# Keys loaded ahead of queries, and 154 of the first 345 steps of a hand-ordered program moved

## The chip, the core and the metric

The kernel runs on one core of a Trainium2 chip. Its time is device microseconds of one execution; 244.88 us is the median of three runs (244.7 to 245.37). A profiled execution gives the trace that is read here.

## What is computed

Attention with squared sketches, and behind it a feed-forward block that multiplies two projections. Cut to its core:

```python
# q, k, v: (4, 4, 1088, 32); S1, S2: (8, 32)
def phi(x):
    a = np.einsum('rd,bhsd->bhsr', S1, x)
    b = np.einsum('rd,bhsd->bhsr', S2, x)
    return np.einsum('bhsi,bhsj->bhsij', a, b).reshape(*x.shape[:-1], 64)
q_p, k_p = phi(q), phi(k)
kv = np.einsum('bhsf,bhsd->bhfd', k_p, v)
z = np.sum(k_p, axis=2)
x = einsum('bhsf,bhfd->bhsd', q_p, kv) / (einsum('bhsf,bhf->bhs', q_p, z)[..., None] + 1e-6)
x = x.transpose(0, 2, 1, 3).reshape(4352, 128)
out = (((x @ w1) * (x @ w2)) @ w3) @ w_out        # w1, w2: 128 x 1024; w3: 1024 x 1024; w_out: 1024 x 128
```

S and the weights come as float64 words, which the kernel turns into float32 itself.

## The kernel before

The program is a list of 1179 named steps. `make_steps` defines each step as a function that issues a few instructions; the text `ORDER` names the steps one by one, and each engine (and each of the queues that issue DMAs, SP's and ScalarE's) gets its instructions in that order. An engine never passes an instruction that waits. Buffers are handed out in the same order: `SLOTS` says, tag by tag, which of the buffers each allocation takes, so a load into a buffer waits for the last reader of what was there. DMAs take eight completion counters in turn, and one that takes a counter again waits for the landing of its former user. Of the large loads at most four (`UNDER_WAY`) are outstanding.

Names: a prefix says whose step it is, then a dot, then what it does.

- `s.*`: the sketch matrices. `s.load`, `s.words` (ScalarE, L263 and L295), `s.pair`, `s.lead`, `s.sum` (DVE), `s.low`, `s.rest` (POOL), `s.T`, `s.P`, `s.R` (TensorE), `s.tc`, `s.Pc`, `s.c` (ScalarE); `s.blk` and `s.blkh` spread them over heads on POOL, into `RS` and `Rh`.
- `k0` to `k3`: keys of the four batches. `k0.load0` and `k0.load1` are issued on ScalarE's queue (two heads each), `k0.loadr` (the last 64 rows) on SP's. `max` is a sum of absolute values on ScalarE (L207) that sets a grid, `g` adds its two halves, `lead` rounds to the grid (L214 on DVE, L211 and L212 on ScalarE), `rest` subtracts (L651). `tr` transposes (TensorE, L685), `kT` copies the transposed keys, `ab` and `abc` make the sketches, `kp` their products (L677). `gram0` to `gram4` add up keys' inner products in `ps_g` (L659). From it, `Gm`, `Gt`, `Ga`, `Gb`, `Gc`, then `T0`, `T1`, `Ta`, `Tb`, `Tc`, then `N0`, `N1`, `Na`, `Nb` find the denominator's matrix, alternately on TensorE and DVE; `Nh` and `Nf` spread it over heads (POOL). `kv0` to `kv3` and `kvr` add up kv in `ps_kv` (L769, L776); `kvm`, `kzt`, `kz`, `kvc`, `kqt`, `kq` bring it into the forms that queries meet.
- `kr0`, `kr1`: the last 64 rows of keys of two batches at a time.
- `q0` and `q1`: the first two groups of 512 queries (batch 0). `tr` (DVE, L1000) turns them, `restT` takes the remaining columns (L979), `max`, `l2`, `l1` (ScalarE) and `rm` (DVE) cut them into two parts. `A0`, `C0` (numerator side) and `A1`, `C1` (denominator side) are products; `C1` of `q0` gives `ps_cy`, which `C1t` turns into `ay_C` (L1068). `sm`, `st`, `sh`, `sl`, `sc` with a or y, `al`, `p01`, `p2`, `p12`, `dn`, `de`, `rc` end in `s_rc`, one over the denominator; `phi`, `pt`, `pc`, `x`, `xc`, `xs`, `xt`, `xT` make the group's `xT`.
- `w0` to `w10`: weights; `load`, `c` and `m` on ScalarE, `j` on DVE, `a` on POOL.
- `g0` to `g7`, `gr`: the feed-forward block by groups of 512 tokens: `a` and `b` (TensorE, L1799 and L1809), `c` (copy, L1804), `m` (product, L1815), `o`.
- `warm0` to `warm11`: products of zeros with zeros (L255), `WARM` gives their counts. They keep TensorE at work while it has nothing else.

An fp32 product is two matmuls and two weight loads on TensorE; one of zeros (bf16) is one of each.

Of the kernel before, what the change touches and what calls it, by code (L numbers as in the profile page):

```python
# [72 lines left out]


ORDER = """
c.zeros warm0 q0.load c.ident s.four c.act c.mask s.zero k0.zero v0.zero s.load k0.load0 k0.loadr q0.restT q0.tr
k0.load1 s.words kr0.load k0.tr1 s.pair s.low s.lead s.sum k0.max0 k0.max1 warm1 q0.max k0.tr0 warm2 kr0.tr kr0.kT
warm3 s.rest w1.load s.T s.P s.tc warm4 q0.l2 k0.kT1 s.Pc s.R k0.g k0.lead0 s.c s.blk k0.rest0 q1.tr k0.gram0 s.blkh
k1.zero s.Pm warm5 q0.l1 q0.A0 warm6 kr0.ab k0.lead1 q0.rm q0.sma q0.sta warm7 k0.kT0 v0.load v0.loadr k1.load k0.ab1
q0.sha k0.rest1 q0.C0 k0.gram1 k0.gram2 k0.gram3 k0.gram4 k0.ab0 k0.abc1 q1.max q0.C0t q0.sla q1.l2 k1.loadr s.Pp  # L80
k0.Gm k0.Gt k0.Ga w1.c1 k0.Gb k0.abc0 k0.T0 q1.l1 warm8 kr0.abc k0.kp1 q0.sca w1.j1 k0.Ta k0.kp0 k0.Gc w1.c0 k1.tr0
kr1.load k2.zero k1.tr1 k1.kT1 kr0.kp warm9 k0.N0 warm10 k0.Na warm11 k0.T1 k0.kv0 k0.Tc k0.Tb k0.N1 k0.Nb k0.Nh q1.rm
q0.al k0.Nf q0.phi0 q0.phi1 q0.A1 q0.smy w1.m1 k1.max q0.sty q0.shy k0.kv3 k0.kv1 k0.kv2 q0.sly s.KS k0.kvr kr1.tr
k0.kvm w1.m0 kr1.kT q0.p01 q1.C0 q1.C1 q0.C1 k0.kzt k2.loadr q0.pt0 q0.C1t q0.scy q0.p2 k0.kz q0.pt1 k0.kvc kr1.ab
k0.kqt q0.p12 q0.dn q0.de q0.rc w1.j0 q0.pc0 q0.pc1 q0.x0 k1.kT0 q0.x1 q0.xs0 q0.xs1 q0.xt0 w1.a0 q1.A0 k2.load
w0.load k1.lead0 q0.xc0 q0.xc1 k0.kq w1.a1 k2.max q0.xt1 k1.ab q0.xT0 q0.xT1 g0.4a q1.load g0.5a q1.sm w0.m1 q1.st
q1.Ct g0.4c g0.4b q1.sh q1.sl k1.rest0 g0.7b w0.c1 g0.7a k1.abt w0.j1 k1.gram0 w0.c0 s.RC q1.scy k1.gram1 kh2.load
q1.sca q2.tr g0.5c q1.al q1.p01 q1.p2 k1.gram2 k1.gram3 kr1.abc k1.gram4 w6.load w0.m0 g0.6b w0.j0 g0.7c g0.7m k1.Gm
q1.p12 k1.Gc g0.0a w2.load w0.a1 q1.dn q1.de q1.rc q1.bs k1.Gt g0.3a k1.Ga k1.T0 k2.kT1 k1.Gb g0.3c q1.restT g0.2a
q1.phi k1.T1 q1.pt0 g0.4m w0.a0 q2.max q2.l2 g0.6a k1.Ta k2.lead0 k2.rest0 g0.1a g0.2c k1.Tc g0.5b q3.tr g0.5m k1.Tb  # L90
q1.pc0 q1.pt1 g0.1b w9.load k1.N0 s.AR q2.l1 q2.rm v3.zero q1.pc1 k1.N1 q1.x g0.6c g0.1c k1.Na k1.Nr k3.zero k2.gram0
g0.1m k2.gram1 k2.gram2 q3.max k2.gram3 g0.0c k2.kT0 k1.Nb q1.xT k2.gram4 q3.l2 k2.ab q2.A0 q2.C0 q2.C1 q3.l1 k1.kp0
v1.zero w9.c k2.abt g1.5a g1.5c g1.1a q2.Ct g1.7a q2.At q3.rm q3.A0 k0.Nr q2.sm q3.C0 q3.C1 k2.Gm v1.loadr q2.st w2.m
q2.sh g1.1c g1.2a k1.kp1 g0.6m q3.Ct g1.0a g1.7b k3.load v1.load g1.5b q3.At k2.Gt k3.loadr w2.c k2.Ga g0.0b w9.j
q2.sl g1.7c w6.c g1.6a k1.kv0 q3.sm k2.Gb w5.load q2.sc q2.al g1.0c k2.Gc g1.7m q2.p01 q3.st k1.kv2 k1.kv3 q3.sh w9.m
k1.kv1 k2.T0 k1.kvr q3.sl q2.p2 k2.T1 q2.p12 q2.dn q2.de g1.4a q2.rc k3.max g0.3b g0.0m g1.1b kh3.load g1.4c k2.Ta
g1.2b q3.sc g1.2c w5.c k2.Tc k1.kvc k1.kqt k1.kq g0.3m q3.p01 g1.6c g1.3a g1.5m g1.3b q2.bs q2.phi0 q2.pT0 g1.2m g1.3c
q2.x q2.load k2.N0 k2.Tb k3.lead0 w9.a1 k2.N1 g1.4b q3.al q3.p2 q3.p12 q2.xT0 g2.5a k3.kT1 g2.5c g2.6a q3.dn q3.de
# [51 lines left out]
def make_steps(ctx, tc, q, k, v, S1, S2, moe_w1, moe_w2, moe_w3, moe_w_out, out):  # L150
    nc = tc.nc
    dve, act, pe, pool, sp = nc.vector, nc.scalar, nc.tensor, nc.gpsimd, nc.sync
    B, H, S, D = q.shape
# [96 lines left out]
    def warm(name, times, tag="out"):  # L250
        @step(name)
        def _():
            t = ps(tag, [128, 256], "idle_ps")
            for _ in range(times):
                pe.matmul(t, zeros, bview(zeros, [[0, 2], [1, 128]]), start=True, stop=True)  # L255

# [586 lines left out]
    def k_end(b):  # L843
        a = acc[b]
        tag = "t"

# [63 lines left out]
        def by_head(o, P, x, start, stop):  # L910
            for h in range(H):
                pe.matmul(o[h * D:(h + 1) * D], P, a["Tp"][:, x, h], start=start, stop=stop,
                          tile_position=(0, h * D), skip_group_check=True)
# [1021 lines left out]
```

## Time and profile before

| | |
|---|---|
| median of three runs | 244.88 us (244.7 to 245.37) |
| profiled execution, span | 244.1 us |
| instructions in the span | 6745 |
| TensorE, DVE, ScalarE, POOL busy | 97%, 85%, 51%, 66% |
| moved by DMA | 22.06 MB, mean 90 GB/s |

The span runs from the first to the last instruction of one execution; the page gives no other time of that execution. The runs' times include what lies ahead of the first and behind the last instruction: the median is 0.78 us above the span. The page has the engines' busy time, the span in 40 slices (6.1 us each), the DMA queues, and the chain that ended last; further answers of the trace give instructions in order of time, waits, and the sums of chosen stretches (for each engine busy time, and in brackets the count of instructions).

### The profile page before, as it was taken

The numbers are of one execution on the slowest core, as the hardware profiler recorded it, in microseconds if no ns is written. First come the engines' busy times: TensorE is split into PE (matmuls) and PEld (weight loads), VectorE is DVE, ScalarE is ACT, GpSimd is POOL, SyncE is SP. The second block draws the span as 40 slices with busy tenths as digits, with TensorE's granted clock in tenths as the row PEclk, the third lists the DMA queues.
The fourth block names the chain that finished last, engine by engine and source line by source line (L and its number), as shares of the span: only waits on it lengthen the run. The fifth ranks groups of instructions, "written<-read, shape, count | busy, mean of one in ns | idle before, by whom it ended". The sixth has DMA issues, their size and how long they took to land.

```text
span 244.1 us, 6745 instructions
## 1 busy us (share of the span) xinstructions
PE 236.2 (97%) x2724; PEld 129.8 (53%) x2724; DVE 206.7 (85%) x421; ACT 123.5 (51%) x246; POOL 161.9 (66%) x203
## 2 busy tenths in 40 slices
...
GB/s 201 265 143 325 181 227 190 6 197 224 220 141 251 188 217 190 59 1 3 3 0 0 4 0 3 59 113 3 1 0 0 0 3 0 0 1 3 12 90 93
DMA packets 31935, 22.06 MB, mean 90 GB/s; under 512 B 21280, under 2 KB 26528, under 8 KB 31904
## 3 DMA queue, kind: packets, MB, share of 16 engines
...
q8 instruction: 21, 0.34, 0.6%
...
q14 instruction: 10, 0.08, 0.1%
...
## 4 chain that ended last, share of the span: by engine, by line
PE 87%; DMA 5%; ACT 2%; POOL 2%; DVE 1%; issue 1%; POOLq 0%; SPq 0%
PE b_ps L1809 12%; PE ps_o L1835 12%; PE ps_X L1673 11%; PE a_ps L1799 11%; PE ps_o L1759 10%; PE ps_w3o L534 6%; PE ps_Y L1673 6%; PE ps_Z L1673 3%; PE ps_g L659 2%; PE ps_x L1527 2%; PE ps_ac L1374 2%; DMA qh<-in_q_dram 2%; DMA k<-in_k_dram 2%; PE ps_or L1824 2%; POOL ph L1208 1%; PE idle_ps L255 1%
## 5 line engine op out<-in xcount | busy, mean ns | idle before, releaser
L1673 PE MATMUL ps_X<-xd,wv 64*128 64x512 f32 x112 | 36.3, 593 | 0.0
L1799 PE MATMUL a_ps<-xT,w 128*128 128x512 f32 (+1 forms) x80 | 36.1, 562 | 0.0
L1809 PE MATMUL b_ps<-xT,w 128*128 128x512 f32 (+1 forms) x80 | 35.6, 555 | 0.0
L1804 ACT COPY ffa<-a_ps 128x512 f32<-128x512 f32 (+1 forms) x38 | 20.1, 540 | 29.2 <-PE a_ps L1799 26.7
L1707 POOL TENSOR_TENSOR hc<-hc 128x512 f32<-128x512 f32 x16 | 20.7, 1304 | 15.7 <-DVE hc L1685 15.5
L1835 PE MATMUL ps_o<-ab,w3o 128*128 128x512 f32 x64 | 29.6, 600 | 0.0
L1680 ACT COPY hc<-ps_X 128x512 f32<-128x512 f32 x38 | 21.3, 590 | 16.1 <-PE ps_X L1673 12.9
L1815 DVE TENSOR_TENSOR ab<-ffa,b_ps 128x512 f32<-128x512 f32 (+1 forms) x40 | 23.9, 623 | 4.9 <-PE b_ps L1809 4.1
L501 POOL TENSOR_TENSOR w3c<-w3c,cv_m 128x512 int32<-128x512 int32 x16 | 21.2, 1344 | 4.2 <-DVE w3c L495 4.1
L1673 PEld LDWEIGHTS ps_X<-xd,wv 64*128 64x128 f32 x112 | 14.9, 186 | 13.1 <-issue 10.9
L1799 PEld LDWEIGHTS a_ps<-xT,w 128*128 128x128 f32 x80 | 14.1, 189 | 13.9 <-issue 8.8
L1809 PEld LDWEIGHTS b_ps<-xT,w 128*128 128x128 f32 x80 | 14.4, 190 | 13.1 <-issue 8.1
L1673 PE MATMUL ps_Y<-xd,wv 64*128 64x512 f32 x48 | 19.7, 594 | 0.0
L1835 PEld LDWEIGHTS ps_o<-ab,w3o 128*128 128x128 f32 x64 | 11.6, 190 | 13.4 <-issue 13.0
L534 PEld LDWEIGHTS ps_w3o<-wo,w3T 128*128 128x128 f32 x128 | 15.3, 192 | 2.4 <-issue 2.4
L534 PE MATMUL ps_w3o<-wo,w3T 128*128 128x128 f32 x128 | 15.7, 276 | 0.0
L1759 PE MATMUL ps_o<-hc,w3o 128*64 128x512 f32 x32 | 15.1, 595 | 0.0
L1759 PE MATMUL ps_o<-tt,ws 128*64 128x512 f32 x32 | 13.7, 594 | 0.0
L1680 ACT COPY hc<-ps_Y 128x512 f32<-128x512 f32 x14 | 8.1, 592 | 9.7 <-PE ps_Y L1673 6.6
L263 ACT ACTIVATE cv_c<-raw 128x1024 f32<-128x1024 f32 (+1 forms) x13 | 13.0, 1014 | 0.0
L1540 ACT COPY xd<-ps_x 64x256 f32<-64x256 f32 x24 | 8.8, 367 | 7.2 <-PE ps_o L1835 6.8
...
## 6 DMA issues: line engine op xcount, KB each, us to landing
...
```

Source lines behind the costliest of these rows:

```text
L263: act.activation(dst, hi.bitcast(F32), ACT.Prelu, scale=2.0 ** -112, alpha=-2.0 ** 32)
L501: pool.tensor_tensor(d, d, x["m"][:, i * 512:(i + 1) * 512], ALU.add)
L534: pe.matmul(t["o"], w3T[ko][:, c], wo[:, c], start=c == 0, stop=c == NC - 1)
L1673: pe.matmul(x[bank], stat(j, u)[:, i * 128:(i + 1) * 128], rows(j, u), start=new, stop=True, tile_position=(u * 64, 0), skip_group_check=True)
L1680: cp(n(y))(x[k], x[bank])
L1707: on(f"h{g}.{i}m{k}").tensor_mul(both[0][k], both[0][k], both[1][k])
L1759: pe.matmul(acc_o[bank][half[0]:half[1]], w(i), x(i), start=n == 1, stop=n == (2 if j == 3 else 4), tile_position=(0, half[0]), skip_group ...
L1799: pe.matmul(x["a"][:, :w], w_of(0, c), xT[g][:, c0:c0 + w], start=True, stop=True)
L1804: cp(f"g{g}.{c}{su}c")(x["s"][:, :w], x["a"][:, :w])
L1809: pe.matmul(x["b"][:, :w], w_of(1, c), xT[g][:, c0:c0 + w], start=True, stop=True)
L1815: dve.tensor_mul(ab_sb[g, c][:, c0:c0 + w], x["s"][:, :w], x["b"][:, :w])
L1835: pe.matmul(o_ps[g], w3o[:, c], ab_sb[g, c], start=n == 1, stop=n == NC)
```

## The change

The order of the steps up to the 345th of 1179 is another one; none is added or taken out. Keys of batch 0 are loaded first, queries of batch 0 behind S. The zero products ahead of everything become 44 of 32 weight columns by 96 columns, instead of 27 of 128 by 256. `SLOTS` is rewritten so that buffers follow the new order. The list `CPV` loses three names whose steps are DVE transposes either way, and `two`'s users no longer write a name that `T1` and `N1` write. The diff, with the middle of the order cut:

```diff
-WARM = [27, 2, 3, 4, 4, 4, 1, 2, 1, 1, 2, 2]
+WARM = [44, 2, 3, 4, 4, 4, 1, 2, 1, 1, 2, 2]
...
 ORDER = """
-c.zeros warm0 q0.load c.ident s.four c.act c.mask s.zero k0.zero v0.zero s.load k0.load0 k0.loadr q0.restT q0.tr
-k0.load1 s.words kr0.load k0.tr1 s.pair s.low s.lead s.sum k0.max0 k0.max1 warm1 q0.max k0.tr0 warm2 kr0.tr kr0.kT
-warm3 s.rest w1.load s.T s.P s.tc warm4 q0.l2 k0.kT1 s.Pc s.R k0.g k0.lead0 s.c s.blk k0.rest0 q1.tr k0.gram0 s.blkh
-k1.zero s.Pm warm5 q0.l1 q0.A0 warm6 kr0.ab k0.lead1 q0.rm q0.sma q0.sta warm7 k0.kT0 v0.load v0.loadr k1.load k0.ab1
-q0.sha k0.rest1 q0.C0 k0.gram1 k0.gram2 k0.gram3 k0.gram4 k0.ab0 k0.abc1 q1.max q0.C0t q0.sla q1.l2 k1.loadr s.Pp
-k0.Gm k0.Gt k0.Ga w1.c1 k0.Gb k0.abc0 k0.T0 q1.l1 warm8 kr0.abc k0.kp1 q0.sca w1.j1 k0.Ta k0.kp0 k0.Gc w1.c0 k1.tr0
-kr1.load k2.zero k1.tr1 k1.kT1 kr0.kp warm9 k0.N0 warm10 k0.Na warm11 k0.T1 k0.kv0 k0.Tc k0.Tb k0.N1 k0.Nb k0.Nh q1.rm
-q0.al k0.Nf q0.phi0 q0.phi1 q0.A1 q0.smy w1.m1 k1.max q0.sty q0.shy k0.kv3 k0.kv1 k0.kv2 q0.sly s.KS k0.kvr kr1.tr
-k0.kvm w1.m0 kr1.kT q0.p01 q1.C0 q1.C1 q0.C1 k0.kzt k2.loadr q0.pt0 q0.C1t q0.scy q0.p2 k0.kz q0.pt1 k0.kvc kr1.ab
-k0.kqt q0.p12 q0.dn q0.de q0.rc w1.j0 q0.pc0 q0.pc1 q0.x0 k1.kT0 q0.x1 q0.xs0 q0.xs1 q0.xt0 w1.a0 q1.A0 k2.load
-w0.load k1.lead0 q0.xc0 q0.xc1 k0.kq w1.a1 k2.max q0.xt1 k1.ab q0.xT0 q0.xT1 g0.4a q1.load g0.5a q1.sm w0.m1 q1.st
+c.zeros warm0 k0.zero k0.load0 k0.loadr k0.load1 c.act s.load s.zero v0.zero c.ident s.four q0.load c.mask warm9
+s.words k0.max0 s.pair k0.tr1 warm1 s.lead s.low s.sum kr0.load warm4 k0.max1 k0.kT1 q0.tr w1.load s.rest warm5 s.P
+s.T kr0.tr s.tc k0.tr0 q0.max q0.restT k0.g s.R warm2 warm3 kr0.kT q0.l2 q1.tr k0.lead0 k0.rest0 s.c s.Pc k1.zero s.Pm
+q0.l1 k0.lead1 s.blk warm6 warm7 s.blkh kr0.ab q0.A0 q0.sma q0.sta k0.ab1 k0.gram0 q0.rm k1.load k0.rest1 v0.load
+q0.sha v0.loadr k0.gram1 q0.C0 k0.gram2 k0.gram3 k0.kT0 k0.abc1 k0.gram4 q1.max k0.ab0 q0.sla q1.l2 q0.C0t k1.loadr
+k0.Gm k0.Gt s.Pp w1.c1 k0.Ga k0.Gc warm8 k0.Gb k0.T0 kr0.abc q1.l1 k0.kp1 q0.sca k0.Ta w1.j1 k0.abc0 kr0.kp k0.Tb
+k0.T1 k0.kp0 w1.c0 kr1.load warm11 k1.tr1 k0.Tc k0.N0 k0.N1 warm10 k0.Na k1.kT1 k2.zero k1.tr0 k0.Nh k0.Nb k0.Nf q1.rm
+q0.al q0.phi0 kr1.tr q0.phi1 q0.A1 k0.kv0 k1.max q0.smy w1.m1 q0.sty k0.kv3 k0.kv1 q0.shy k0.kv2 q0.sly s.KS k0.kvr
+w1.m0 kr1.kT k0.kvm q0.C1 q1.C0 k0.kzt q0.C1t k2.loadr q0.pt0 q0.p01 q0.scy q0.pt1 k0.kz q0.p2 k0.kvc q0.p12 kr1.ab
+k0.kqt q0.dn q0.pc0 q0.de q0.rc w1.j0 w0.load q0.pc1 q0.x0 k1.kT0 q0.x1 q0.xs0 q0.xc0 q0.xt0 w1.a0 k2.load q0.xs1
+k0.kq w1.a1 q1.A0 q0.xt1 q0.xc1 q1.C1 k2.max k1.lead0 k1.ab q0.xT0 q0.xT1 g0.5a q1.load g0.4a q1.sm q1.st q1.Ct w0.m1
...
@@ the stretch of TensorE around the gram of batch 2
-q1.pc0 q1.pt1 g0.1b w9.load k1.N0 s.AR q2.l1 q2.rm v3.zero q1.pc1 k1.N1 q1.x g0.6c g0.1c k1.Na k1.Nr k3.zero k2.gram0
-g0.1m k2.gram1 k2.gram2 q3.max k2.gram3 g0.0c k2.kT0 k1.Nb q1.xT k2.gram4 q3.l2 k2.ab q2.A0 q2.C0 q2.C1 q3.l1 k1.kp0
+q2.l1 k1.Tb g0.1b g0.0c k1.N0 v3.zero w9.load s.AR k1.N1 g0.1c q2.rm k1.Na g0.6c q1.pc1 k1.Nr k3.zero k2.gram0 g0.1m
+k2.gram1 k2.gram2 q3.max q1.x k2.kT0 k2.gram3 k2.ab q1.xT q3.l2 k1.Nb g0.6m q3.l1 q2.A0 q2.C0 k2.abt k1.kp0 q2.C1
+g1.5a q2.Ct g1.1a g1.5c w9.c g1.0a q2.At k2.gram4 k0.Nr q3.rm q2.sm q3.A0 q3.C0 q2.st q3.C1 w2.m k2.Gm g1.7a q2.sh
...
         def _():
             t = ps(tag, [128, 256], "idle_ps")
+            if name == "warm0":
+                for _ in range(times):
+                    pe.matmul(t[:32, :96], zeros[:, :32], zeros[:, :96], start=True, stop=True)
+                return
             for _ in range(times):
                 pe.matmul(t, zeros, bview(zeros, [[0, 2], [1, 128]]), start=True, stop=True)
...
-            a["T"], a["Tr"] = two([D, H, r], "ps_T")
+            a["T"], rest = two([D, H, r], "ps_T")
+            if rest is not None:
+                a["Tr"] = rest
```

The same edit as the last stands in `N0`.

More of the change, by code (lines that the diff above doesn't have):

```diff
@@ L29 @@
     "b":
-        "012345670214657210671306537457462512346127340273014526045721472352140327540542370673245716"
+        "051226075314671250467315463470267152346127340270315426045721742351240327540642375072345716"
         "210605643174306437107523543106572361507514502371054643535436051532410354273245554744570504"
@@ L34 @@
     "l":
-        "0123456789a7486797c0864b7705995a34210b38c73b92bc0b4879c146a281ba56271a564b60303643a19ca32c"
+        "1023456879a7486797c0684b7705995a34210b38c73b92bc0b4879c146a281ba56271a564b60303643a19ca32c"
         "c2076b",
     "m":
-        "0123456789aejo96p3ke3rfjo7p5t8g50lfin6q8o4donmgp19fh2og3hi5601au6v4jm8emhubcusv62jgo6olsjs"
+        "2013456789aeoj9p63k3frejo7g5pt850qlifn68o4donmgp19fh2og3hi5601au6v4jm8emhubcusv62jgo6olsjs"
         "aolp8s0h8roj26gk1ivl8hb3mcu0a5pn7tfd9qe0umb4p5j1e2tkmgjeno5rcub7tjkume92fka4ud5tkbigpq10lv"
@@ L42 @@
     "raw": "010212120211221",
-    "s": "012345671252360063202461521024214",
-    "x": "012012201110",
+    "s": "012354671252360063202461521024214",
+    "x": "120012201110",
 }
-WARM = [27, 2, 3, 4, 4, 4, 1, 2, 1, 1, 2, 2]
+WARM = [44, 2, 3, 4, 4, 4, 1, 2, 1, 1, 2, 2]
 BY_PE = ()
@@ L65 @@
 CPV = set("""
-    g0.0c g0.1c h4.1ac h4.1ad h6.1bc h6.2ad k0.kT1 k1.kvc k2.kT1 k2.kq k3.kT0 k3.kT1 k3.kq q0.xc0
-    q0.xc1 q6.xT0 q6.xT2
+    g0.0c g0.1c h4.1ac h4.1ad h6.1bc h6.2ad k0.kT1 k1.kvc k2.kq k3.kq q0.xc0 q0.xc1 q6.xT0 q6.xT2
 """.split())
@@ L86 @@
-w0.load k1.lead0 q0.xc0 q0.xc1 k0.kq w1.a1 k2.max q0.xt1 k1.ab q0.xT0 q0.xT1 g0.4a q1.load g0.5a q1.sm w0.m1 q1.st
[L87 to L90, printed above, removed]
@@ L91 @@
-q1.pc0 q1.pt1 g0.1b w9.load k1.N0 s.AR q2.l1 q2.rm v3.zero q1.pc1 k1.N1 q1.x g0.6c g0.1c k1.Na k1.Nr k3.zero k2.gram0
-g0.1m k2.gram1 k2.gram2 q3.max k2.gram3 g0.0c k2.kT0 k1.Nb q1.xT k2.gram4 q3.l2 k2.ab q2.A0 q2.C0 q2.C1 q3.l1 k1.kp0
-v1.zero w9.c k2.abt g1.5a g1.5c g1.1a q2.Ct g1.7a q2.At q3.rm q3.A0 k0.Nr q2.sm q3.C0 q3.C1 k2.Gm v1.loadr q2.st w2.m
-q2.sh g1.1c g1.2a k1.kp1 g0.6m q3.Ct g1.0a g1.7b k3.load v1.load g1.5b q3.At k2.Gt k3.loadr w2.c k2.Ga g0.0b w9.j
-q2.sl g1.7c w6.c g1.6a k1.kv0 q3.sm k2.Gb w5.load q2.sc q2.al g1.0c k2.Gc g1.7m q2.p01 q3.st k1.kv2 k1.kv3 q3.sh w9.m
+c.zeros warm0 k0.zero k0.load0 k0.loadr k0.load1 c.act s.load s.zero v0.zero c.ident s.four q0.load c.mask warm9
```

9 lines of the change are left out of this document (8 added, 1 removed).

## The prediction

> **What bounds the kernel now.** I read the sums by engine first, then stretches of the span, then the chain of waits.
>
> ```profile
> PE 236.2 (97%) x2724; PEld 129.8 (53%) x2724; DVE 206.7 (85%) x421; ACT 123.5 (51%) x246; POOL 161.9 (66%) x203
> PE 87%; DMA 5%; ACT 2%; POOL 2%; DVE 1%; issue 1%; POOLq 0%; SPq 0%
> 30.00:60.00 30.00, 28.60 (x620) 15.43 (x619) 26.92 (x76) 20.17 (x38) 15.68 (x20) 1.00 0.67 169
> 60.00:100.00 40.00, 40.00 (x541) 22.54 (x541) 37.00 (x68) 24.08 (x43) 33.10 (x26) 1.00 0.81 198
> ```
>
> TensorE is busy all of 60 to 100 us; ahead of that it isn't, and all moved steps lie there. The 834 steps behind the moved ones are in the old order, so what arrives earlier at about 55 us should end the span earlier by as much. The question is how much earlier that is. Its first 30 us are set by a chain over all engines, so I follow that chain by rows of the timeline (start, duration, engine; in brackets the idle time ahead).
>
> ```profile
> 0.74 0.41 SPq L975 DMA_DIRECT2D qh<-in_q_dram  x1
> 0.98 0.95 ACTq L560 DMA_DIRECT2D k<-in_k_dram  x2
> 4.64 0.24 DVE L979 STREAM_TRANSPOSE qT_rest<-qh 128x64 f32<-128x64 f32 x1 [3.70 <-DMA qh<-in_q_dram]
> 4.81 0.67 DVE L1000 STREAM_TRANSPOSE qT<-qh 128x512 f32<-128x512 f32 x1
> 6.18 0.44 PE L685 MATMUL ps_kt<-ident,k 128*128 128x128 f32 x2 [0.28 <-DMA k<-in_k_dram]
> 6.41 0.68 ACT L207 ACTIVATE k_abs<-k 128x576 bf16<-128x576 f32 x1 [0.87 <-POOL sk_m L313]
> 7.76 0.61 ACT L207 ACTIVATE q<-qT 128x512 f32<-128x512 f32 x1
> 8.09 0.55 DVE L214 TENSOR_SCALAR kk<-k,k_g 128x512 f32<-128x512 f32 x1
> 8.66 0.69 DVE L651 TENSOR_TENSOR kk<-k,kk 128x512 f32<-128x512 f32 x1
> 9.27 0.70 DVE L1000 STREAM_TRANSPOSE qT<-qh 128x512 f32<-128x512 f32 x1
> 11.10 0.83 ACT L212 ACTIVATE kk<-kk,k_g 128x640 f32<-128x640 f32 x1
> 11.96 0.82 DVE L651 TENSOR_TENSOR kk<-k,kk 128x640 f32<-128x640 f32 x1
> 14.91 0.19 DVE L217 TENSOR_REDUCE G_g<-ps_g 128x1 f32<-128x32 f32 x1 [1.35 <-PE ps_g L659]
> 16.52 0.18 DVE L204 SCALAR_TENSOR_TENSOR T_p<-T_g,T_t 32x32 f32<-32x32 f32 x1
> 16.63 1.21 DVE L677 TENSOR_TENSOR kp<-kab 128x1024 f32<-128x1024 f32 x1
> 17.76 0.15 DVE L217 TENSOR_REDUCE N_g<-ps_N 128x1 f32<-128x8 f32 x1
> 18.96 0.16 DVE L937 TENSOR_TENSOR RC<-RC,ps_Nr 128x8 f32<-128x8 f32 x1 [0.41 <-PE ps_Nr L912]
> 19.20 0.67 POOL L949 TENSOR_TENSOR RS<-RC,mask 128x64 f32<-128x64 f32 x1
> 21.53 0.29 DVE L1097 TENSOR_TENSOR s_loy<-ps_ay,s_hiy 128x128 f32<-128x128 f32 x1
> 23.20 0.32 DVE L1068 STREAM_TRANSPOSE ay_C<-ps_cy 128x128 f32<-128x128 f32 x1 [1.38 <-PE ps_cy L1030]
> 25.55 0.71 ACT L1280 COPY xs<-s_rc 128x256 f32<-128x256 f32 x2
> ```
>
> Queries land at 4.64, keys at 6.18. ScalarE then works through keys' maximum (6.41), queries' maximum (7.76) and the second half of the keys' leading parts (to 11.93); DVE makes their rest (11.96), TensorE the gram, DVE the chain from G (14.91) to N (to 19.12), and the queries of group 0 wait 1.38 us for ps_cy.
>
> TensorE also has three waits put down to nothing but "issue". The next lines are instructions of TensorE counted from the start (products, then weight loads), pieces of the chain of waits around those waits, a row of the timeline, and two lines of the page:
>
> ```profile
> 0.00:13.80 13.80, 12.52 (x221) 10.28 (x221) 7.93 (x24) 9.07 (x23) 7.20 (x41) 1.00 0.85 239
> 0.00:19.45 19.45, 17.76 (x345) 14.54 (x346) 11.82 (x40) 13.25 (x33) 10.89 (x47) 1.00 0.75 214
> 0.00:45.80 45.80, 42.63 (x850) 29.05 (x851) 34.15 (x97) 32.71 (x74) 27.38 (x66) 1.00 0.75 205
> 12.07 0.79 PE ps_c L1030 x24
> 12.87 1.00 PE ps_g L659 x48
> 13.86 0.41 issue
> 14.27 0.58 PE ps_g L659 x23
> 20.35 0.69 PE L769 MATMUL ps_kv<-kp,v 128*32 128x64 f32 x34 [0.91 <-issue]
> 42.90 0.36 PE ps_N L912 x32
> 43.26 1.01 PE ps_x L1297 x4
> 45.83 1.16 issue
> q8 instruction: 21, 0.34, 0.6%
> GB/s 201 265 143 325 181 227 190 6 197 224 220 141 251 188 217 190 59 1 3 3 0 0 4 0 3 59 113 3 1 0 0 0 3 0 0 1 3 12 90 93
> ```
>
> They fall behind 221 + 221 = 442, 691 and 1701 instructions of TensorE: 249 apart, then 1010, which is four times 252. The instruction queue moved 0.34 MB in 21 packets, one per 16 KB. So code comes in blocks of some 250 instructions, and a block that is used up too fast costs a wait: 0.41 + 0.91 + 1.16 = 2.48 us in all.
>
> **Keys first (k0.load0, k0.loadr, k0.load1 ahead of q0.load).** The same bytes move, so the pair should end as now, at about 6.1; the first of it landed 4.64 - 0.74 = 3.9 us after its issue, so keys come at about 4.4 to 4.6, 1.6 earlier, and queries at 6.0, 1.4 later. k0.loadr stands ahead of S and q0 on SP's queue (small rows, 0.1 us or so); POOL's three fills ahead of ident cost it about 0.6 us, covered until the keys land. The keys' two maxima now run while ScalarE waits for queries (4.0 to 5.4 instead of 6.41 to 7.76). But q0.tr and q0.restT stand ahead of k0.g on DVE, and nothing there may pass them: q0.tr 6.0 to 6.65, restT to 6.85, k0.g 7.0, q1.tr (0.70) 7.65, lead0 8.2, rest0 8.9, where it ends at 9.35 now. ScalarE starts q0.max at 6.65 instead of 7.76; the same work follows, so k0.lead1 ends at 11.93 - 1.1 = 10.8. DVE's own queue ahead of k0.rest1 (q0.sma, sta, rm) is through at about the same time, an estimate; with 0.15 for it rest1 starts at 10.95 instead of 11.96. **Gain 1.0.**
>
> **Gram and G.** q0.C0 (48 of TensorE's instructions, 0.79 us on the chain) moves from ahead of gram1 to behind it, k0.gram0 behind k0.ab1: the sum is the same. gram1 starts 0.7 behind rest1's start, now (12.7) as then (11.65); 1.00 + 0.58 of gram and 0.79 of C0 follow, so the gram would end at 14.0. The first code wait comes at instruction 442 again, which is now the first product of gram3 instead of its middle, since the 17 further zero products (34 instructions) shift all that follows. It ended at 14.27. Its block is ordered once the one before is entered, now in k0.ab1, at 9.1 to 9.7 instead of some 9.5 to 10; so the wait ends about 0.3 earlier, at 14.0, with 96 instructions left instead of 58, some 0.7: end 14.7 if so, 14.0 if the block is there. I take the middle, 14.3, for the end and for Gm, which starts at 14.91 now. **Gain 0.6 stays** (between 0.2 and 0.9).
>
> **From G to N, and POOL.** k0.Ta ahead of w1.j1, k0.T1 and N1 right behind T0 and N0: N1 and Tb no longer stand between N0 and the end, but kp0 (1.2) still stands ahead of Na. From Ta's end (16.70) to RC's (19.12) it is 2.4 us now, with kp0, Na (0.6 with its shifts), Tb and two sums; then w1.j1 and Tb, 0.45, kp0 1.15, Na 0.58, the sums 0.3: 2.5. Nothing. Nf (0.67) moves ahead of q0.al on POOL, so phi0 on DVE, which needs al, starts 0.6 later. s_loy is thus ready at 21.82 - 0.6 + 0.6 = 21.8.
>
> **q0.C1 ahead of q1.C0, q1.C1 behind q1.A0.** ps_cy, made third of three now, is made first: 16 products, against 24 for C0's 0.79, so 0.5 us behind kvr. ps_cy is then there ahead of s_loy, and ay_C starts at 21.8 instead of 23.20. **Gain 1.4**: the idle 1.38 us go. If the second code wait ends as late as now (20.35), the kv products end at 21.1 and ps_cy is there at 21.7: still 1.4. If it ends 1 us later, 0.4 are left.
>
> **Queues that steps are moved past.** v0.load stands behind k1.load on SP, which waits for q1.tr (7.65 instead of 9.98). v0 lands behind w1 and k1: 2.1 MB from 6.1 on, at the 201 to 265 GB/s of the page's first two slices, is 14 to 16.5. kv0 starts at about 18: cover 1.5 us or more; without it, each us costs one. k2.load stands behind w0.load, and k2.max now ahead of k1.lead0 on ScalarE, so that a late k2 would hold up lead0, ffa and w0's words: it is wanted at 25.55 - 1.4 + 1.0 = 25.1, and w0 and k2, 1.6 MB at 265 to 325 GB/s from 16.5 at the latest, land by 22.6. Cover 2.5 us. k1.abt ahead of k1.rest0 on DVE fills the time that lead0 is later by. I cost these at nothing. The renamed buffers, the two rewritten helpers and the shorter list of copies change no instruction.
>
> **The third code wait.** By then 34 instructions more have been issued, and q1.x (1.01) stands behind gram2 instead of ahead of gram0. The block before is entered within N1 (0.36) instead of behind it, so the next comes some 0.4 earlier: 1.16 becomes 0.8. Bounds: it is gone (1.16), or it grows by as much as the longest wait seen (-1.16). I take 0.4. [...]
>
> **Zero products.**
>
> ```profile
> 1.00 4.69 PE L255 MATMUL idle_ps<-zeros 128*128 128x256 bf16 x27 [1.00 <-DVE zeros L229]
> 4.76 0.93 PE L255 MATMUL idle_ps<-zeros 128*128 128x256 bf16 x7
> ```
>
> Twenty of 27 start in the first 3.76 us, seven in the next 0.7: 0.19 to 0.21 us each, then about 0.11. So TensorE runs at half its pace until about 4.4, though the granted clock reads 1.00 in the rows from 0 on. A product of 96 columns is 96/256 of that, 0.08 us, and 44 of them end at about 4.5, as the keys land. Cost nothing, if the pace still changes at 4.4.
>
> **Sum.** 244.1 - 1.4 - 0.4 = 242.3 of span. The median of the runs, 244.88, is 0.78 above this profile's span: 243.1.
>
> **The rivals.**
> 1. The pace changes later. Products of 32 x 96 may not count as work, and behind 4.5 there is little to do until S's parts arrive. Each us that TensorE stays at half pace while it bounds the chain costs up to 0.5. The slow stretch was 3.4 us: one more costs up to 1.7 and gives 244.7; two more cost 3.4 and give 246.4, slower than before. It decides against the gain of 1.8 from 3.6 us on, so at a change behind 8.0. [...]
> 2. Code waits eat the early gain: the first as long as now with more behind it, the second 1 us longer, the third unchanged. 244.1 - 0.4 + 0.78 = 244.5. For it: the second block is fetched while v0, k2 and w0 load. Against: all is ordered earlier.
> 3. The third wait vanishes and queries land at 5.5: 244.88 - 1.9 - 1.16 = 241.8.
> 4. Nothing arrives, as another engine holds the stretch from 30 to 60: DVE is busy 26.92 of 30 there. But DVE too starts it earlier. 244.9.
>
> **How the numbers follow.** Forecast 0.50, 243.1 (242.3 to 243.9). Rival 3: 0.13. Rival 2: 0.13, at the edge between faster and same. Rival 1: 0.15, of which 0.08 with one stretch more (no change) and 0.07 with two. Rival 4: 0.09. A measurement of this kernel tells about 0.3% (0.7 us) from no change. Faster: 0.50 + 0.13 + half of rival 2 = 0.70; slower: 0.07 and 0.03 for a worse code wait = 0.10; same 0.20. The range leaves out two stretches of half pace and the best of rival 3: 241.5 to 245.2.
>
> **What would show it.** Right: keys' transposes at 4.5 and q0.tr at 6.0; G_g at about 14.3; no wait ahead of ay_C, which starts below 22; TensorE's waits for issue below 2.4 in sum; xs at about 24.2. Wrong: TensorE's zero products still 0.08 apart at 5 us, ScalarE waiting for k2 ahead of k1.lead0, kv waiting for v0, or a code wait over 1.5 us at a new place.

## The result, and the profile after

The changed kernel takes 248.78 us (median of 6 runs, 246.74 to 250.03) against 245.07 before; the ratio is 1.0143, interval 1.0108 to 1.0178. It is 1.4% slower, where 243.1 and faster was forecast. Times in this document are medians of all runs, and ratios compare fast runs alone (those within 1.5% of a kernel's shortest) with runs of the kernel before from the same round (medians 244.95 to 245.5), so the two differ a little where runs spread (e6, e10, e14, e18).

The page of the changed kernel: sums by engine, the granted clock in 40 slices, shares of the chain.

```profile
span 245.0 us, 6783 instructions
PE 236.0 (96%) x2741; PEld 130.6 (53%) x2741; DVE 207.0 (85%) x421; ACT 123.4 (50%) x246; POOL 161.6 (66%) x203
PEclk9997999999999999999999999999999999999999
PE 91%; DVE 3%; DMA 2%; issue 1%; SPq 1%; POOL 0%; ACT 0%; DVEq 0%
```

Two stretches of its span (busy time of each engine, then granted clock, DMA share, GB/s; a packet counts whole where it starts, so a share can pass 1):

```profile
30.00:60.00 30.00, 29.98 (x596) 15.90 (x598) 26.71 (x77) 21.42 (x38) 16.13 (x22) 1.00 0.71 172
60.00:100.00 40.00, 40.00 (x577) 22.50 (x566) 36.93 (x68) 24.10 (x43) 33.04 (x27) 1.00 0.84 211
```

From 30 us on TensorE hardly waits any more (29.98 of 30). The loss lies ahead of that, and there one slice of the clock reads 7. The chain's steps in the timeline of the changed kernel:

```profile
4.38 0.62 PE L688 MATMUL ps_kt<-ident,k 128*128 128x128 f32 x4
7.22 0.69 DVE L1007 STREAM_TRANSPOSE qT<-qh 128x512 f32<-128x512 f32 x1
8.05 0.18 ACT L349 COPY sk_t<-ps_st 32x32 f32<-32x32 f32 x1 [1.27 <-PE ps_st L344]
8.13 0.62 ACT L206 ACTIVATE q<-qT 128x512 f32<-128x512 f32 x1
11.26 0.83 ACT L211 ACTIVATE kk<-kk,k_g 128x640 f32<-128x640 f32 x1
12.20 0.88 DVE L654 TENSOR_TENSOR kk<-k,kk 128x640 f32<-128x640 f32 x1
12.91 1.98 POOL L680 TENSOR_TENSOR kp<-kab 128x1024 f32<-128x1024 f32 x1 [0.53 <-ACT kab L711]
12.99 2.04 DVE L203 SCALAR_TENSOR_TENSOR s_hla<-s_ga,s_t 128x128 f32<-128x128 f32 x1
15.73 0.28 PE L662 MATMUL ps_g<-kk 128*32 128x64 f32 x4 [1.78 <-issue]
16.56 0.19 DVE L216 TENSOR_REDUCE G_g<-ps_g 128x1 f32<-128x32 f32 x1 [0.85 <-PE ps_g L662]
21.00 0.16 DVE L944 TENSOR_TENSOR RC<-RC,ps_Nr 128x8 f32<-128x8 f32 x1
24.38 0.31 DVE L1075 STREAM_TRANSPOSE ay_C<-ps_cy 128x128 f32<-128x128 f32 x1
26.81 0.40 ACT L1287 COPY xs<-s_rc 128x256 f32<-128x256 f32 x1 [0.74 <-DVE s_rc L1205]
```

Keys are there at 4.38, as forecast, but the keys' leading parts end where they did (11.26 + 0.83), and in the gram TensorE waits 1.78 us for nothing but its own instructions, where it waited 0.41. Two stretches of 3.41 us around it; the clock's record changes at 17.44 and back at 20.85:

```profile
14.03:17.44 3.41, 1.71 (x56) 1.67 (x55) 2.36 (x7) 1.10 (x5) 1.31 (x2) 1.00 0.18 27
17.44:20.85 3.41, 3.41 (x53) 2.61 (x51) 2.69 (x11) 2.50 (x6) 0.84 (x3) 0.50 0.46 101
```

TensorE is idle in half of the first, and has half its clock (0.50) in the second. This was the shortest of the six runs. A second trace (e12 below, 248.49) stands for the median. Its span with the mean granted clock:

```profile
core 0: 246.7 us, clock 0.985
```

The wait in the gram, in its timeline:

```profile
16.06 0.28 PE L654 MATMUL ps_g<-kk 128*32 128x64 f32 x4 [2.28 <-issue]
```

And three stretches of 3.41 us; here the clock's record changes at 17.26 and back at 24.08:

```profile
13.85:17.26 3.41, 1.20 (x51) 1.16 (x51) 0.40 (x3) 0.98 (x2) 1.60 (x2) 1.00 0.13 18
17.26:20.67 3.41, 3.41 (x37) 2.65 (x40) 2.18 (x9) 2.01 (x7) 0.83 (x2) 0.50 0.42 87
20.67:24.08 3.41, 3.41 (x95) 3.23 (x91) 2.58 (x9) 2.91 (x6) 2.20 (x4) 0.50 0.93 273
```

(Lines in the kernels of the experiments lie some 8 lower.) A second trace of the kernel before (e5) has a span of 243.3 at a time of 245.08, 1.78 apart; every run here with both numbers has 1.7 to 1.9. So the page of before, 244.1 long, shows an execution of about 245.9, and the 0.78 compared two different executions. The forecast isn't off by that, as it comes to 244.88 less the gains. I compare with e5 from here. Start times in us, from the timelines ("held" is e17 below):

| step | e5, before | after | e12, after again | e17, held |
|---|---|---|---|---|
| code block ahead of the gram's border entered | 10.09 | 11.02 | 10.90 | 10.82 |
| fetch of the next block starts | 11.67 | 13.29 | 13.58 | 11.25 |
| wait at that border | 0.34 | 1.78 | 2.28 | under 0.3 |
| G_g | 14.94 | 16.56 | 16.89 | 15.52 |
| RC, last sum | 18.99 | 21.00 | 21.80 | 19.53 |
| xs | 25.04 | 26.81 | 27.81 | 25.32 |
| last store issued | 240.14 | 241.81 | 243.53 | 240.63 |

From e5 to e12 the end moves by 3.39. Of this 1.95 is there at G_g, as much as the wait grew (2.28 - 0.34 = 1.94), and another 0.86 at RC, where TensorE has half its clock. The last 0.58 come behind RC and were not traced.

### The profile page after: what moved, and what is told of

The parts are those of the page before. It is cut to its first block, busy times and chain, and to the rows that moved or that the text cites. A ratio compares the mean times of both kernels' runs of the same rounds, so it can differ in the third digit from the quotient of the medians.

```text
span 245.0 us, 6783 instructions
## 1 busy us (share of the span) xinstructions
PE 236.0 (96%) x2741; PEld 130.6 (53%) x2741; DVE 207.0 (85%) x421; ACT 123.4 (50%) x246; POOL 161.6 (66%) x203
## 4 chain that ended last, share of the span: by engine, by line
PE 91%; DVE 3%; DMA 2%; issue 1%; SPq 1%; POOL 0%; ACT 0%; DVEq 0%
PE a_ps L1806 13%; PE b_ps L1816 13%; PE ps_o L1842 12%; PE ps_X L1680 11%; PE ps_o L1766 10%; PE ps_w3o L537 6%; PE ps_Y L1680 6%; PE ps_g L662 3%; PE ps_Z L1680 3%; PE ps_x L1534 2%; PE ps_ac L1381 2%; DMA kr<-in_k_dram 2%; PE ps_or L1831 2%; PE ps_kv L772 1%; PE ps_ab L705 1%
## 5 line engine op out<-in xcount | busy, mean ns | idle before, releaser
L1680 PEld LDWEIGHTS ps_X<-xd,wv 64*128 64x128 f32 x112 | 14.9, 186 | 13.2 <-issue 10.9
L1806 PEld LDWEIGHTS a_ps<-xT,w 128*128 128x128 f32 x80 | 14.2, 189 | 13.7 <-issue 10.2
L1816 PEld LDWEIGHTS b_ps<-xT,w 128*128 128x128 f32 x80 | 14.3, 190 | 13.3 <-issue 8.3
L1842 PEld LDWEIGHTS ps_o<-ab,w3o 128*128 128x128 f32 x64 | 11.6, 190 | 13.4 <-issue 13.0
L1504 POOL COPY nz<-nz 32x8 f32<-32x8 f32 x32 | 11.1, 347 | 1.4
```

The source lines that it names most:

```text
L1680: pe.matmul(x[bank], stat(j, u)[:, i * 128:(i + 1) * 128], rows(j, u), start=new, stop=True, tile_position=(u * 64, 0), skip_group_check=True)
L1806: pe.matmul(x["a"][:, :w], w_of(0, c), xT[g][:, c0:c0 + w], start=True, stop=True)
L1816: pe.matmul(x["b"][:, :w], w_of(1, c), xT[g][:, c0:c0 + w], start=True, stop=True)
L1842: pe.matmul(o_ps[g], w3o[:, c], ab_sb[g, c], start=n == 1, stop=n == NC)
```

## The experiments

**Where the borders of the code lie.** Counted with TensorE's semaphore instructions, the waits for issue of before stand at its instructions 448, 704 and 1728, all of the form 192 + 256 n. Theory 1 makes them the cause: a block's code comes late, TensorE idles, and then the clock is halved. Theory 2 puts the loss on the order itself, theory 3 on the zero products as too little work for the clock. The first runs move the borders and nothing else.

e1, the changed kernel: `WARM = [44, ...` to `[76, ...`, and 48 columns for 96.

> The changed kernel with 76 zero products of 48 columns in place of 44 of 96: about the same time on TensorE, 64 instructions more ahead of everything else. Theory 1 (a late code block, then half pace): TensorE enters the block that ends with instruction 442 some 64 instructions further up, at 6 to 8.5 us instead of 10.96, so the next block is there before it is reached; the wait of 1.78 us in the gram is under 0.3, G_g starts at 15.6 to 15.8 (then held by DVE, not TensorE), no half-pace stretch at 17 to 21 us, mean granted clock 0.997 or more in every run, xs on ScalarE at 25.0 to 25.7 instead of 26.81, time 243.5 to 245.5. Theory 2 (the new order itself is longer, the code wait only lies in a gap): xs at 26.5 or later, time as the changed kernel's, 246.5 to 250. Theory 3 (narrow zero products are too little work for the clock): clock 0.985 or less, time over 248.

e2, the kernel before: `WARM = [27, ...` to `[13, ...`, with 512 columns each.

> The kernel before with 13 zero products of 512 columns in place of 27 of 256: the same time on TensorE, 28 instructions fewer ahead of everything else, order untouched. Theory 1: the block is entered 28 instructions further down, at about 11.2 us instead of 10.02; 4.2 to 4.8 us from entry to use put the end of the wait at 15.4 to 16.0 against a boundary reached at about 14.1: a wait of 1.0 to 1.8 us in gram4 or behind it, instead of 0.41, and with it a half-pace stretch near 17 to 21 us in at least some runs (mean clock 0.993 or less there); time 245.5 to 248.5. Theory 2: no part of the new order is in it, so 244.6 to 245.3. Theory 3: more columns per product, so no loss of pace, 244.6 to 245.3.

e3, the kernel before, with the changed kernel's `WARM = [44, ...` and narrow warm0.

> The kernel before with the 44 narrow zero products of the changed one, order untouched. Theory 1: the block is entered at about 9.7 and the boundary reached at about 13.4; the first wait stays at 0.3 to 0.9, the clock at 0.997 or more; the later boundaries lie 34 instructions further up, so the third wait (1.16) may shrink: time 243.7 to 245.3. Theory 2: 244.6 to 245.3. Theory 3: the clock rises later than 4.3 us or falls again behind it, mean clock 0.993 or less, time 246.5 or more.

e4, the changed kernel:
```diff
-... s.blk warm6 warm7 ... k0.ab1 k0.gram0 q0.rm
+... s.blk k0.gram0 warm6 warm7 ... k0.ab1 q0.rm
```

> The changed kernel with k0.gram0 moved back ahead of the zero products behind s.blk, so that its 64 instructions run at about 9.9 us, ahead of k0.ab1 as in the kernel before, and not at 11.9. Theory 1: the block is entered at about 10.0 instead of 10.96; the wait of 1.78 us shrinks to 0.3 to 1.2, the half-pace stretch is gone in most runs, time 244.5 to 246.5. Theory 2: one step among 154, the time stays at 246.5 to 250. Theory 3: the same zero products, so the same loss of pace: 246.5 to 250.

All four are slower than the kernel before: 250.63 (ratio 1.0219, 1.0184 to 1.0254), 251.98 (1.0283, 1.0252 to 1.0314), 246.95 (1.0093, 1.0058 to 1.0129) and 248.24 (1.0138, 1.0115 to 1.0161). All four lie above the range that theory 1 had given, so what speaks for it is where the waits stand, and not the times. TensorE's longest wait for issue in e1, in the view of waits (sum, times, longest):

```profile
PE ps_c L1029 <- issue: 2.6, 1, 2.6
```

Those of e2:

```profile
PE ps_kv L762 <- issue: 3.8, 1, 3.8
PE ps_g L652 <- issue: 1.9, 2, 1.1
```

Those of e3:

```profile
PE ps_krab L825 <- issue: 1.9, 1, 1.9
PE ps_g L655 <- issue: 1.1, 2, 0.6
PE a_ps L1795 <- issue: 1.0, 1, 1.0
```

And e3's span and clock:

```profile
core 0: 244.9 us, clock 1.000
```

In e1 the wait in the gram is gone, and one of 2.6 stands at the next border but one (960), with half pace behind it: the wait is moved, not removed. Its clock also fell for one stretch at 9.76, ahead of any code wait (ten zero products take 2.29 us from 9.69, 1.27 in the changed kernel); whether so many small products bring that was not separated, so theory 3 may hold for e1. e2 and e3 keep the old order and lose 7.0 and 2.0 us by 28 instructions fewer and 34 more; in e3 at full clock, with 4.0 us of waits at borders in the profiled run against 1.6 in e5. So theory 3 falls for the change's own zero products: they cost by their number of instructions. e4 misses: the block is entered at 10.51, but its fetch starts only at 14.17, and the wait is 2.35.

**The parts of the order.** e5 is the kernel before, unchanged; e6 the changed order with the old 27 zero products (`WARM = [44, ...` to `[27, ...`, 256 columns); e7 the kernel before with one move; e8 the changed kernel with warm2, warm3, warm6 and warm7 as 36 products of 72 columns, not 10 of 256.

> The kernel before, unchanged, for a second trace with its own time beside it. Theory 1 (waits at the borders of TensorE's code blocks, every 256 instructions): waits for issue again at the same instruction counts (442, 691, 1701) and nowhere else, each different by up to 1 us from the first trace, because the fetch starts when the bulk loads leave room; no half-pace stretch. If the time less the span is near 1.8 us as in the other runs, a typical span of this kernel is 243.1 and the page's 244.1 was a long one.

> The changed kernel with the old zero products (27 of 256 columns): the order alone, 34 instructions fewer ahead of everything. Theory 1: the border at instruction 442 now lies 34 instructions further down, in gram4 or k0.ab0; the block ahead of it is entered behind the start of gram0, at about 11.9, and used up in 2 to 2.5 us where the fetch takes 4.2 to 4.8: a wait of 1.8 to 2.8 us, half pace behind it in most runs, time 247.5 to 251. Theory 3 (the narrow zero products do the harm by themselves): clock 0.997, time 243 to 245. Theory 2 (the order is longer apart from code): 246 to 249 with a code wait under 1 us.

e7:
```diff
-... q1.C0 q1.C1 q0.C1 k0.kzt
+... q0.C1 q1.C0 q1.C1 k0.kzt
```

> The kernel before with one step moved: q0.C1 ahead of q1.C0 and q1.C1, instead of behind them; no instruction more or less, so the borders of the code blocks stay up to that place and behind it. If the prediction's largest term holds: ay_C starts at 21.6 to 22.0 instead of 23.20 without idle time ahead of it, xs at 24.2 to 24.6 instead of 25.55, time 243.4 to 244.2. Theory 1 adds that the stretch from instruction 691 to the next border gets shorter by as much, so that up to 1 us of it may come back as a wait at about instruction 942 (no wait there before): 243.4 to 245.0. Rival (DVE and TensorE are held elsewhere by 50 us): 244.7 to 245.2.

> The changed kernel with 36 zero products of 72 columns in place of the 10 of 256 that run between 9.5 and 10.6 us: about the same time on TensorE, 52 instructions more ahead of ps_krab, the 44 narrow ones as in the changed kernel. Theory 1: by the changed kernel's trace without its waits, the blocks that end with instructions 442, 691 and 942 then last 5.6, 4.6 and 3.8 us (2.7, 5.9 and 6.0 there), so the wait of 1.78 in the gram is gone, gram ends at 14.7 to 15.0, no half pace at 17 to 21; a wait of 0 to 2 us may stand at 942, near 24 us, with half pace behind it if it is over 1.5; time 243.5 to 247.5. Theory 2 (the order itself): xs not ahead of 26.5, 246.5 to 250. Theory 3: the same narrow products and more of them, so 248 or more.

e6 takes 249.99 (1.0194, 1.0154 to 1.0234), with waits of 1.81 and 1.84: the order loses without the new zero products too. e7 takes 245.02 (0.9994, 0.9979 to 1.0009). Its timeline, DVE's row and TensorE's longest wait:

```profile
21.57 0.31 DVE L1060 STREAM_TRANSPOSE ay_C<-ps_cy 128x128 f32<-128x128 f32 x1
46.83 0.19 PE L651 MATMUL ps_g<-k,kk 128*32 128x32 f32 x1 [1.97 <-issue]
```

In the timeline of e5:

```profile
22.69 0.32 DVE L1060 STREAM_TRANSPOSE ay_C<-ps_cy 128x128 f32<-128x128 f32 x1 [0.82 <-PE ps_cy L1022]
```

The forecast's largest term works in its place (ay_C 1.12 earlier, no idle time), 0.46 of it reaches xs (24.58 against 25.04), and the third border takes that back: TensorE comes there 0.44 earlier, its code comes 0.5 later (fetch at 44.38 against 43.85), and the wait is 1.97 against 0.87. The queues were 0.83 busy from the entry of the block ahead (42.11) to that fetch, in e5 0.05 (from 42.55). This trace is of the longest of e7's 12 runs (245.76), so it shows this wait at its worst; the median says that no gain is left at the end.

e8 takes 248.95 (1.0166, 1.0132 to 1.0201). The block is entered at 9.62, the fetch starts at 10.06, and no wait is left in the gram; G_g comes at 15.83, so 0.7 of the first trace's loss there was the wait and 0.9 the order. Then 2.27 us are lost at border 960, and a half-pace stretch behind it, so the time misses theory 1's range and lies in theory 2's.

**Other causes in the order, and fewer loads.** e9 is e8 with q0.sha moved ahead of k0.rest1 on DVE. e10 and e11 set `UNDER_WAY = 4` to `2`, in the kernel before and the changed one. e12 is the changed kernel again.

> The kernel of the 26 further products with one more step moved: q0.sha (a SCALAR_TENSOR_TENSOR of DVE, 0.29 us by itself) ahead of k0.rest1, as in the kernel before, so that it runs ahead of GpSimd's k0.kp1 and not beside it, where it took 2.04 us. Theory 2 (part of the loss is the order itself, at this place): G_g starts at 14.9 to 15.2 instead of 15.83, and 0.6 to 0.9 of it reaches the queries' sums (s_loy at 22.1 to 22.4 instead of 23.00). Theory 1: what is gained there is met again at the border at instruction 942, whose code comes when it comes (fetch at 22.57): the wait there grows from 2.3 to about 3; time 248 to 249.5, no better than without the move. If code waits didn't take it back: 247.9 to 248.4.

> The kernel before with at most 2 bulk loads under way in place of 4; the same instructions. Theory 1, with bulk loads as the reason why code comes late: the fetches of the code blocks start within 1 us of the entry of the block ahead (1.3 to 3.0 now), the three waits (0.5, 0.6, 1.1) shrink to under 0.5 in sum, time 243.3 to 244.6, provided that the data still come in time. Rival (the fetch is late by itself, whatever the loads do): the same waits, and the loads end later: 245 to 250, with TensorE or ScalarE waiting for DMA.

> The changed kernel with at most 2 bulk loads under way in place of 4. Theory 1, with bulk loads as the reason: fetch 2.3 us behind the entry falls to under 1, the wait of 1.78 in the gram to 0.3 to 0.8, half pace is rare, G_g at 15.7 to 15.9 (DVE's order holds it there), time 245 to 247. Rival (late by itself): waits and clock as in the changed kernel, 248 to 252 as data come later too.

> The changed kernel, unchanged, for a second trace: its first had one half-pace stretch and was the shortest of 6 runs (246.74), the median 248.78. Theory 1: a time near 248.7 comes with the code wait in the gram again (1.5 to 2.5 us) and two half-pace stretches, or with further waits at later borders; the steps of DVE and ScalarE up to 11.9 us as in the first trace.

e9 takes 249.85 (1.0165, 1.0116 to 1.0214): q0.sha runs in 0.34 us, but the fetch comes 2.44 us behind the entry this time (queues 0.85 busy in the 0.4 us behind the entry, 0.36 in e8), TensorE waits 1.00 in the gram and 3.38 at border 960. e10 and e11 are far slower as wholes, 261.24 and 261.41, since from 50 us on TensorE waits for v (6.9 and 5.5 us). Ahead of that e10 shows what was asked: the fetch for 448 starts at 10.35, 0.46 behind the entry, that for 704 costs no wait either, and G_g comes at 14.22, 0.72 ahead of e5; the third border, at 44.8, still costs 1.43. In e11 the fetch still came 2.0 late, with a wait of 1.40: its queues were 0.89 busy in the 0.4 us behind the entry, in e10 0.15.

**Why the code comes late.** The fetch for 448 starts at 11.6 to 11.8 in e2, e3, e5 and e7, whether the block was entered at 9.7 or at 10.9; with the changed order at 13.3 to 14.2 (after, e4, e6, e12). Theory 4: it gets through when the DMA queues have a gap. e13 takes v0's load back to its place, e14 adds two more moves, e15 moves v0's load alone in the kernel before, e16 sets `UNDER_WAY` to 3 there.

```diff
e13  -... k1.load k0.rest1 v0.load q0.sha v0.loadr    +... v0.load v0.loadr k1.load k0.rest1 q0.sha
e14  e13, with q0.sha ahead of k0.rest1, and  -k0.Nf q1.rm q0.al  +q1.rm q0.al k0.Nf
e15  -v0.load v0.loadr k1.load k0.ab1 q0.sha k0.rest1    +k1.load k0.ab1 q0.sha k0.rest1 v0.load v0.loadr
```

> The changed kernel with v0.load and v0.loadr moved back ahead of k1.load, their place before; nothing else. Theory 4 (v0 behind k1 fills the DMA queues when TensorE asks for code): v0 goes out at 5.3 to 6.8, the queues have a gap near 11 to 12 us as in the kernel before, the fetch starts at 11.0 to 12.2 instead of 13.3 to 13.6, the wait in the gram is 0 to 0.9 instead of 1.8 to 2.3, half pace behind it is gone in most runs, G_g at 15.2 to 15.9 instead of 16.6 to 16.9, time 244.8 to 246.8. Rival (the place of v0's load doesn't matter, as the sum says that cost it at nothing): fetch at 13 or later, wait 1.5 or more, time 248 to 249.5.

> The kernel of the run before with two more steps moved back: q0.sha ahead of k0.rest1 (so that DVE isn't held by GpSimd's k0.kp1) and k0.Nf behind q0.al on GpSimd. Theory 4 with Theory 2 for the rest: G_g 0 to 0.5 earlier than in the run before, s_loy another 0.5 earlier; if the later borders leave it, time 0.3 to 1.0 below the run before, 244.0 to 246.0, which would be the first version level with the kernel before or better. If the gain is met at a later border: within 0.4 of the run before.

> The kernel before with v0.load and v0.loadr moved behind k0.rest1, so behind k1.load as in the changed kernel; nothing else. Theory 4: v0 goes out at 9 to 11 instead of 5.5, DMA queues full from 11 to 14, the fetch for instruction 442 starts at 12.5 to 14.2 instead of 11.7, the wait there is 1.2 to 2.8 instead of 0.4 to 0.5, half pace behind it in part of the runs, time 246 to 249. Rival: fetch at 11.7 as ever, wait under 0.8, time 244.6 to 245.6.

> The kernel before with at most 3 bulk loads under way in place of 4. Theory 4: queues less full, so the first two waits (0.5 and 0.6) shrink to 0 to 0.3 each and the gram is 0.3 to 0.6 earlier, as with 2 loads, where all that was lost again at 50 us on v's load coming 6.9 us late; with 3 that should be 0 to 2 us: time 244.0 to 246.5.

The place of v0's load as the cause falls. e13 takes 248.44 (1.0115, 1.0071 to 1.0159): k1 and its rows fill the queues from 9 to 13.5 instead, the fetch starts at 13.94, the wait is 2.63. e15 goes the other way than expected, 245.38 (0.9995, 0.9972 to 1.0018): without v0 the queues are 0.28 to 0.43 busy from 9.5 to 11.5, the fetch starts at 10.77, and the waits at 448 and 704 are both gone; the border at 46 us takes the gain back (1.65). e14, at 248.06 (1.0073, 1.0036 to 1.0110), keeps its wait in the gram (1.84), and its runs spread from 245.4 to 253.3. e16 misses, 246.84 (1.0050, 1.0019 to 1.0081): its fetch starts at 11.54, but takes 2.54 us instead of about 1.1, and TensorE waits 1.32. What is left of theory 4 is the gap itself. e17 makes one, without a change of order, instructions or borders; e18 adds q0.sha and k0.Nf as in e14.

```diff
+        if name == "s.blk":
+            gate = [i for i in traced[n:] if i.engine == nc.gpsimd.engine][-1]
+        if name == "k1.load":
+            for i in traced[n:]:
+                if i.engine == nc.sync.engine:
+                    tc.add_manual_dep(i, gate.name, landed, reason="gate")
```

> The changed kernel with one wait more: k1.load on SP waits for GpSimd's s.blk (end 10.3), so that k1, v0 and k1's rows go out some 1.5 us later; order, instructions and borders unchanged. If full DMA queues are what delays the code: the queues are less than 0.6 busy from 10 to 11.5, the fetch asked for at 10.9 starts at 11.0 to 12.0 instead of 13.3 to 13.6, the wait in the gram is 0 to 0.6 instead of 1.8 to 2.3, no half pace at 17 to 21, G_g at 15.0 to 15.9, time 245.0 to 246.8. If not: fetch at 13 or later, wait over 1.5, time 248 to 249.5. k1 and v0 are wanted at 18 us and later and should not be missed.

> The same with q0.sha ahead of k0.rest1 and k0.Nf behind q0.al. G_g at 14.8 to 15.2, s_loy at 21.3 to 22.0, xs at 24.0 to 24.8, time 243.6 to 245.6: level with the kernel before or up to 0.5% faster, if the wait at about 46 us does not take the gain back as it did in e7 and e15; if it does, 245 to 246.

e17 takes 246.25 (1.0026, 1.0002 to 1.0049): with one wait more on SP, the changed kernel gets back most of what it had lost. Two stretches of the changed kernel (the last two numbers: DMA share, GB/s):

```profile
10.00:11.50 1.50, 1.50 (x20) 1.44 (x17) 0.64 (x4) 1.47 (x3) 1.34 (x5) 1.00 0.83 282
11.50:13.20 1.70, 1.70 (x89) 1.63 (x91) 1.70 (x4) 1.70 (x4) 1.09 (x3) 1.00 1.03 332
```

The same of e17:

```profile
10.00:11.50 1.50, 1.42 (x17) 1.19 (x14) 0.82 (x5) 1.47 (x3) 1.34 (x5) 1.00 0.27 70
11.50:13.20 1.70, 1.70 (x97) 1.63 (x100) 1.70 (x3) 1.70 (x5) 1.04 (x3) 1.00 0.74 198
```

The packet of TensorE's code (queue q8: packets, MB, share; its 21 packets for TensorE's 5482 instructions are one per 261) in the DMA view of the changed kernel from 13.2 to 13.4 us; there is none from 10.9 to 13.2:

```profile
q8 instruction: 1, 0.02, 33.1%
```

The same view of e17, from 11.1 to 11.4 us:

```profile
q8 instruction: 1, 0.02, 25.8%
```

And e17's span and clock:

```profile
core 0: 243.8 us, clock 1.000
```

Both enter the block at about 10.9. With queues 0.83 and then 1.03 full the packet starts 2.3 us later; with 0.27 it starts at 11.25, 0.4 later, there is no wait over 0.3 in the gram, and the clock stays (of the twelve runs, one has 0.986, the others 0.997 or more). e18 takes 245.80 (1.0023, 0.9995 to 1.0051), no better than the kernel before: no version beat it. It misses its G_g (15.31): q0.sha takes 0.34 us, but the packet of code takes 1.83 us instead of 1.24, and TensorE waits 0.82 in the gram.

All 20 traces agree with e17 at this border. In the five whose queues were 0.08 to 0.44 busy in the 0.4 us behind the entry (e8, e10, e15, e17, e18), the fetch started 0.4 to 0.7 us behind it; in the other fifteen, with 0.73 or more, 0.9 to 3.7 us. At the next border, 704, quiet queues are not enough: in e6 TensorE had the block ahead from 16.62, the queues were 0.08 busy, and the fetch started at 19.02. There it starts 98 to 105 instructions into the block in 13 of the 20 traces, and no run shows why.

## Why the prediction was wrong, step by step

- **Gram and G: the step that failed.** It took the block to be entered "in k0.ab1, at 9.1 to 9.7" and the fetch to follow at a fixed distance, so that the first wait ends at 14.0 and G_g comes 0.6 earlier. The block was entered at 11.0, since k0.ab1 started at 10.88 (11.14 in e5) and gram0's 64 instructions now ran behind it; and the distance isn't fixed (1.58 in e5, 2.27 and 2.68 in the two traces of the changed kernel). The wait ended at 15.73 and 16.06, and G_g came 1.62 and 1.95 later than in e5. e17 shows the distance as the cause: the same entry, order and instructions, and some 2 us less wait.
- **Queues that steps are moved past: "I cost these at nothing".** The cover for v0 and k2 was there: TensorE nowhere waits for them. But k1.load went out at 8.73 instead of 10.01, with v0 and k1's rows right behind, and TensorE's code had to pass that; e17 holds back just these. No step of the sum looked at what else uses the queues.
- **Rival 1 named the second half of the loss in the wrong place.** It had half pace at 1.7 us a stretch, from a late start of the clock behind the zero products. The stretches came at 17 to 24 us, behind the code wait. A late start there was as well, in e12: the four transposes of the keys take 1.06 us at 4.81, where the first trace has 0.62 at 4.38; but the block was entered at 10.90, no later than there (11.02), so it cost nothing by then. Rival 2 had code waits that eat the gain, without the clock, and so ended at 244.5. The outcome is both: the wait and then its stretches.
- **Keys first, gain 1.0: nothing.** q0.tr ran at 7.22, not at 6.0: the work on S's words (5.33 to 6.70) and k0.kT1 stand ahead of it on DVE. q0.max ran at 8.13 (7.76 before), behind sk_t on ScalarE, which waits 1.27 us for ps_st. S's words land at 5.0 as before and end in RS at 9.88 (9.81 before); that chain bound the stretch, and the working left it out.
- **q0.C1 first, gain 1.4:** right in its place (1.12 in e7), 0.46 at xs, nothing at the end. "What arrives earlier at about 55 us should end the span earlier": what arrives earlier at 42 us waits for code at 46.
- **From G to N: nothing, and phi0 0.6 later:** held. RC comes 4.0 behind G_g in e8 and in e17, 4.05 in e5; s_loy 3.17 behind RC in e8, 2.58 in e5.
- **The third code wait, 1.16 to 0.8:** none in the first trace of the changed kernel and 0.76 in e12, against 1.16 and 0.87 in the two of the kernel before, so this term was about right. One crossing of a border cost up to 3.8 us (e2).
- **Zero products: no cost by their time,** as forecast (end at 4.34); but their 34 instructions alone cost the old order 2.0 us (e3).
- **One loss isn't in the sum: DVE beside GpSimd.** q0.sha moved behind k0.rest1 and now meets k0.kp1. In the first trace k0.kp1 starts at 12.91 (1.98 us) and q0.sha, at 12.99, takes 2.04 us; in e12 q0.sha is first (12.94 against 12.98) and takes 0.28. Behind k0.kp1 it takes 2.04 in e8 and 2.08 in e17 too, and 0.28 in e13, where both start at 12.92. What the two engines share these rows do not show. While the code wait is there it hides this; in e8 and e17 it doesn't, and G_g comes at 15.83 and 15.52. In e17 the gram is over at 14.6, and DVE has no idle time between these rows:

```profile
12.84 2.08 DVE L195 SCALAR_TENSOR_TENSOR s_hla<-s_ga,s_t 128x128 f32<-128x128 f32 x1
15.52 0.15 DVE L208 TENSOR_REDUCE G_g<-ps_g 128x1 f32<-128x32 f32 x1
```

What stays open: what e17 still loses (0.26%), of which G_g's 0.58 against e5 is put down to this overlap by the rows alone, since in e18, without it, the code wait was back; why single packets took long (2.54 us in e16, 1.83 in e18); and what holds the fetch for border 704 when the queues are quiet.
